# A recurrent layer followed by a mixture of experts: the first expert is settled in iteration 2, its weights are loaded in iterations 3 to 10, and units 4 and 5 are turned by TensorE

## The chip, the core and the metric

The kernel runs on one core of one Trainium2 chip. The metric is the device time of one execution in microseconds (us), here the median of three runs.

## What is computed

A linear recurrence with decay runs over 4 sequences of 768 tokens with 8 heads of 48 values, and its output (3072 tokens of 384 values) goes through a mixture of 8 experts, one expert for each token:

```python
for t in range(S):                      # recurrence: B 4, H 8, S 768, D 48
    cur = einsum('bhd,bhe->bhde', u * k[t], v[t])
    y[t] = einsum('bhd,bhde->bhe', r[t], state + cur)
    state = w * state + einsum('bhd,bhe->bhde', k[t], v[t])
logits = x @ w_gate + modality_bias[modality_id]   # x: y as 3072 x 384
e_idx = argmax(logits); gate_w = softmax(logits)[e_idx]
out[mask_e] = gate_w * (relu(x[mask_e] @ w1[e]) @ w2[e])   # e of 8, F 1024
```

## The kernel before

The tokens are cut into 24 **units** of 128 (chunk c of sequence b). The loop `for i in range(NU - 1)` in `run` is a software pipeline written out by hand: each engine executes its instructions in the order in which this loop issues them, and there is no scheduler behind it. In iteration i TensorE turns keys of unit i+2 (`keys_turned`, tile pkT), computes the scores of unit i+1 (`scores`, psc), then the output and the state of unit i (`values`, py and pst). VectorE masks scores (`causal`, at), adds the parts of the output of unit i-1 (`token`, py) and makes keys with decay (`keys`, kc). ScalarE copies states (st), scales values (`own`, dv) and makes the sum of squares of `token` (row). GpSimd makes rc, rk and kt. pst has one buffer, so `values` of unit i waits until ScalarE has taken the state of unit i-1 out of it. The psc, pkT and pxT tiles share four buffers.

SyncE (SP) issues the loads: per iteration `turned` (ud, of unit i+5) and `lines` (kv, of unit i+4). All go through one queue, in order, and an entry that waits holds up those behind it. `pace` makes SP wait for a value that VectorE has written.

Each finished unit is turned so that features lie on partitions, for the gate. `flip` does it by a DMA transpose (xT from row). For units in `RAISED`, `raised` does it on TensorE instead, with six 128x128 transposes into pxT two iterations later, and `flipped` copies pxT to xT on ScalarE. `logits` of the first group (units 0 to 3) stands at the end of iteration 5.

The experts' weights are of float32. They come into `raw` in halves of 256 KB (`half`, twelve for the first expert) and need six sums of squares (`norm` q, ScalarE into junk), two scale factors (`scales`, a matmul, a reduction wtotw and three small VectorE operations) and six `split`s: `wide` on ScalarE makes whi, `fine` on VectorE makes wlo. The first expert is chosen before the tokens are counted, by a poll (`first_order`): from the modality of the tokens and the bias it estimates which expert gets most tokens, and writes the order of the experts to `ctl`. SP reads the first of them from there before the first half is loaded.

Small work is threaded between the large by `fill()`: a list of generators of which each call runs one step. There are nine such calls in an iteration. `plan(i, f)` puts f at the end of iteration i, `begin[i]` and `mid[i]` put it inside. O is 8. From iteration 13 on the first expert's products (`s_up`, tile phs; `s_down`, pos) run between the units.

Of the kernel before, what the change touches and what calls it, by code (L numbers as in the profile page):

```python
# [9 lines left out]
F32 = mybir.dt.float32  # L10
# [8 lines left out]
P = 128  # L19
# [3 lines left out]
NT = B * S  # L23
# [25 lines left out]
RAISED = range(6, 12)  # L49
# [16 lines left out]
class _Kernel:  # L66
# [134 lines left out]
    def setup2(self):  # L201
# [10 lines left out]
        pt = self.ps_r.tile([P, 512], F32, tag="r", name="pswg")  # L212
# [19 lines left out]
        mf, mp = pt[:, 64 : 64 + NTT], c.tile([P, 1], F32, name="modp")  # L232
        self.polled = pt, mp, bias
        nc.scalar.activation(mf, mod.rearrange("p (t w) -> p t w", w=2)[:, :, 0], AF.Copy, accum_out=mp)
        yield
# [474 lines left out]

    def first_order(self):

        c, v = self.c, self.nc.vector
        pt, mp, bias = self.polled
        one = slice(0, 1)
        new = lambda name, shape: c.tile(shape, F32, name=name)
        b2 = bias.rearrange("p (m e) -> p m e", m=2)
        n1, rev, best1, perm = new("n1", [P, 1]), new("rev16", [P, E]), new("best1", [P, E]), new("perm0", [P, E, E])
        self.perm0 = perm
        square = lambda ap: ap.rearrange("p (a b) -> p a b", b=E)  # L720
        top, gr = pt[:, 384:386], square(pt[:, 128 : 128 + E * E])
        best0, by, rank, t = (pt[:, o : o + E] for o in range(400, 400 + 4 * E, E))
        self.nc.tensor.matmul(pt[:, 1:2], self.ones, mp, start=True, stop=True)
        v.reduce_max(top, b2, axis=AX.X)
        yield
        self.nc.scalar.activation(rev, self.rev, AF.Copy, scale=1 / 16)
        self.nc.scalar.activation(rev, self.rev, AF.Copy, scale=1 / 16)
        v.tensor_tensor(best0, b2[:, 0], top[:, :1].to_broadcast([P, E]), ALU.is_equal)
        yield
        self.nc.scalar.copy(n1, pt[:, 1:2])  # L730
        v.tensor_tensor(best1, b2[:, 1], top[:, 1:].to_broadcast([P, E]), ALU.is_equal)
        yield
        v.tensor_sub(by, best1, best0)
        yield
        v.scalar_tensor_tensor(best1, best0, float(NT), rev, ALU.mult, ALU.add)
        yield
        v.scalar_tensor_tensor(rev, by, n1, best1, ALU.mult, ALU.add)
        yield
        v.scalar_tensor_tensor(best0, by, n1, best1, ALU.mult, ALU.add)
        yield  # L740
        v.tensor_tensor(gr, rev.unsqueeze(1).to_broadcast([P, E, E]), best0.unsqueeze(2).to_broadcast([P, E, E]), ALU.is_gt)
# [12 lines left out]
        self.nc.scalar.copy(self.ctl[:, :E], eid)  # L754
# [394 lines left out]
    def run(self):  # L1149
# [34 lines left out]
        def half(q):  # L1184
            if q == 0:
                self.eid = nc.sync.value_load(self.ctl[:, :1], min_val=0, max_val=E - 1)
            if 0 <= q < 2 * NQ:
                self.load(self.eid, 2 * NQ, q)
# [12 lines left out]
        plan(1, lambda: fills.append(routing))  # L1201
        plan(3, lambda: fill(99))
        plan(3, lambda: fills.append(self.first_order()))
# [45 lines left out]
        for i in range(NU - 1):  # L1249
# [16 lines left out]
            if i == O + 5:  # L1266
                self.settled_state(i - 1)
# [7 lines left out]
            if i != O + 5:  # L1275
                each(i - 1, self.settled_state)
# [52 lines left out]
            if i != O + 5:  # L1329
                self.values(i)  # L1330
# [229 lines left out]
```

## Time and profile before

| what | value |
|---|---|
| median of three runs | 344.19 us (343.73 to 344.73) |
| the profiled execution | 343.19 us |
| its span, first to last instruction | 341.3 us |
| TensorE matmul busy | 322.7 us, 95% of the span |
| VectorE, ScalarE, GpSimd busy | 213.3, 180.1, 160.5 us |
| granted TensorE clock over the span | 0.997 |

The share of an engine is an average over stages. Busy time of TensorE counts matmuls whose ends are modelled, so that short waits between them hide in it. An iteration is told here from the first scores matmul of one unit to that of the next; iteration 2 begins at 19.52 us, iteration 14 ends at 100.18.

### The profile page before, as it was taken

The numbers are of one execution on the slowest core, as the hardware profiler recorded it, in microseconds if no ns is written. First come the engines' busy times: TensorE is split into PE (matmuls) and PEld (weight loads), VectorE is DVE, ScalarE is ACT, GpSimd is POOL, SyncE is SP. The second block draws the span as 40 slices with busy tenths as digits, with TensorE's granted clock in tenths as the row PEclk, the third lists the DMA queues.
The fourth block names the chain that finished last, engine by engine and source line by source line (L and its number), as shares of the span: only waits on it lengthen the run. The fifth ranks groups of instructions, "written<-read, shape, count | busy, mean of one in ns | idle before, by whom it ended". The sixth has DMA issues, their size and how long they took to land. (4 is left out here: it accounts for less than half of the span.)

```text
span 341.3 us, 15249 instructions
## 1 busy us (share of the span) xinstructions
PE 322.7 (95%) x5459; PEld 262.8 (77%) x5459; DVE 213.3 (63%) x745; ACT 180.1 (53%) x482; POOL 160.5 (47%) x237
## 2 busy tenths in 40 slices
PE   7999998889899999899999999999999999999992
PEld 3788897778778888687887778886888887777771
DVE  7868987489997997587758732268322332334950
ACT  7787788578766568367532222265222224553820
POOL 8978779688739786526268411112122111211211
PEclk9999999999999999999999999999999999999998
DMA  6766999667659999995345632217611121112110
GB/s 187 237 165 161 169 250 301 181 224 169 182 139 234 195 281 285 235 131 147 71 130 175 190 96 65 47 46 249 195 46 46 47 69 23 46 52 64 37 46 5
DMA packets 58013, 47.93 MB, mean 140 GB/s; under 512 B 42344, under 2 KB 50807, under 8 KB 57712
## 3 DMA queue, kind: packets, MB, share of 16 engines
q1 hardware_dynamic: 54768, 37.85, 46.9%
q0 software_dynamic: 3200, 9.47, 7.7%
q8 instruction: 30, 0.49, 0.6%
q14 instruction: 15, 0.12, 0.1%
HBM read 27.21 MB, written 11.83 MB: 114 GB/s over the span
## 5 line engine op out<-in xcount | busy, mean ns | idle before, releaser
L1051 PEld LDWEIGHTS <-whi 128*128 128x128 f16 x1248 | 72.4, 98 | 3.8 <-issue 0.9
L1060 DVE SCALAR_TENSOR_TENSOR hl<-phb,hh 128x256 f16<-128x256 f32 (+1 forms) x48 | 24.4, 508 | 68.3 <-ACTq L1491 68.3
L1114 PEld LDWEIGHTS <-hh 128*128 128x128 f16 x416 | 39.1, 98 | 27.6 <-issue 2.2
L1051 PE MATMUL phb<-mxT,whi 128*128 128x128 f16 x768 | 50.8, 219 | 0.0
L431 ACT ACTIVATE dv<-kv,d 128x48 f32<-128x48 f32 x172 | 43.1, 325 | 0.4 <-DVE d L419 0.2
L1055 ACT ACTIVATE hh<-phb 128x256 f16<-128x256 f32 (+1 forms) x48 | 21.5, 455 | 32.6 <-PE phb L1051 21.9
L1051 PEld LDWEIGHTS <-wlo 128*128 128x128 f16 x624 | 37.7, 98 | 0.0
L1020 POOL TENSOR_TENSOR seenb<-otb,putb 128x1 int32<-128x1 int32 x16 | 4.4, 275 | 64.0 <-ACTq L1491 51.9
L451 DVE TENSOR_TENSOR at<-psc,mask 128x512 f32<-128x512 f32 x48 | 31.9, 682 | 1.9 <-PE psc L445 1.8
L364 POOL TENSOR_TENSOR rc<-ud,powr 112x512 f32<-112x512 f32 (+1 forms) x25 | 31.0, 1243 | 0.7 <-DMA ud<-in_pd 0.5
L1114 PEld LDWEIGHTS <-hl 128*128 128x128 f16 x208 | 19.4, 98 | 15.3 <-issue 2.5
L1011 ACT ACTIVATE otb<-po,fac 128x384 f32<-128x384 f32 x16 | 9.3, 580 | 39.5 <-PE phb L1051 36.1
L688 POOL DMA_INDIRECT rows<-row,posi x24 | 25.0, 1042 | 10.8 <-DVE base L664 3.1
L445 PE MATMUL psc<-rc,kc 64*64 64x128 f32 (+1 forms) x768 | 27.1, 276 | 2.3 <-issue 1.5
L1051 PE MATMUL phb<-mxT,wlo 128*128 128x128 f16 x384 | 29.3, 219 | 0.0
L1114 PE MATMUL po<-whi,hl 128*128 128x384 f16 x136 | 28.0, 326 | 1.2 <-PEq L1556 0.7
L1114 PE MATMUL po<-whi,hh 128*128 128x384 f16 x136 | 27.7, 326 | 0.5 <-ACT hh L1055 0.4
L1114 PE MATMUL po<-wlo,hh 128*128 128x384 f16 x136 | 27.6, 326 | 0.0
L1051 PE MATMUL phs<-mxT,whi 128*128 128x128 f16 x432 | 27.2, 219 | 0.0
L445 PEld LDWEIGHTS psc<-rc,kc 64*64 64x64 f32 (+1 forms) x768 | 20.9, 132 | 7.9 <-issue 4.2
L482 PE MATMUL py<-kv,at 128*64 128x48 f32 x768 | 26.5, 221 | 0.0
L997 DVE SCALAR_TENSOR_TENSOR wlo<-raw,ws,whi 128x1024 f16<-128x1024 f32 (+1 forms) x20 | 25.0, 1277 | 1.4 <-issue 0.6
(287 smaller groups left out, 636.0 us busy)
## 6 DMA issues: line engine op xcount, KB each, us to landing
kv<-in_pt SPq DMA_DIRECT2D x21, 384.0 KB
ud<-in_pd SPq DMA_DIRECT2D x10, 384.0 KB
raw<-in_w SPq DMA_DIRECT2D x12, 256.0 KB
raw<-in_w SPq DMA_DIRECT2D x6, 512.0 KB
raw<-in_w SPq DMA_DIRECT2D x2, 1536.0 KB, 6.3
ud<-in_pd SPq DMA_DIRECT2D x14, 192.0 KB
rows<-pad SPq DMA_DIRECT2D x10, 193.0 KB
rt<-in_pt SPq DMA_DIRECT2D x7, 192.0 KB
```

What stands on the lines that cost most here:

```text
L364: nc.gpsimd.tensor_mul(u["rc"][:TOP, s], u["rT"][:TOP, s], self.powr[:TOP, s])
L431: nc.scalar.activation(u["dv"][:, sl], u["v"][:, sl], AF.Copy, scale=u["d"][:, h : h + 1])
L445: nc.tensor.matmul(u["ps"][j][s, pr * P : (pr + 1) * P], u["kc"][r, pr, s], u["rc"][r, pr, :], start=True, stop=True)
L451: nc.vector.tensor_mul(u["at"][:, j * NPR : (j + 1) * NPR, :], u["ps"][j].rearrange("p (q t) -> p q t", q=NPR), self.mask.unsqueeze(1).to_ ...
L482: nc.tensor.matmul(py[t, sl], u["at"][:, j * NPR + pr, t], u["v"][:, sl], start=c == h == 0, stop=h == H - 1, skip_group_check=True)
L688: i = nc.gpsimd.indirect_dma_start(out=self.rows, out_offset=bass.IndirectOffsetOnAxis(ap=u["posi"][:, b : b + 1], axis=0), in_=u["row"][: ...
L997: self.nc.vector.scalar_tensor_tensor(self.wlo[:, sl], self.raw[:, sl], sc, self.whi[:, sl], ALU.mult, ALU.subtract)
L1011: self.nc.scalar.activation(ot, po[:, :DM], AF.Copy, scale=gf[:, t : t + 1])
L1051: self.nc.tensor.matmul(ph[:, q * P : (q + 1) * P], w[:, c0 : c0 + P], self.xT[:, xq, t * P : (t + 1) * P], start=i == q == 0, stop=i == l ...
L1055: self.nc.scalar.activation(self.hh[:, f0 : f0 + fb, t * P : (t + 1) * P], p3, AF.Relu)
L1060: self.nc.vector.scalar_tensor_tensor(self.hl[:, f0 : f0 + fb, r], p3, 0.0, self.hh[:, f0 : f0 + fb, r], ALU.max, ALU.subtract)
L1114: self.nc.tensor.matmul(po[:, :DM], h[:, f, t * P : (t + 1) * P], w[:, c0 : c0 + DM], start=first, stop=last)
```

## The change

- `RAISED` begins at 4 and not at 6: units 4 and 5 are turned by TensorE in iterations 6 and 7, and their two DMA transposes, in iterations 5 and 6 on SP, go.
- The poll is taken apart. `first()` settles the first expert alone, writes `ctl[0]`, and runs at the head of the chain of small work, from iteration 2 on. The rest of `setup2` follows it, and then the rest of the order. Before, `setup2` came first and the poll began in iteration 4.
- The twelve halves are issued by a table, in iterations 3 to 10 (2, 1, 2, 1, 1, 2, 2, 1); before, two in each of iterations 6 to 11.
- The norms stand in iterations 5, 7, 8, 9, 10 and 11; before in 7 to 12. The splits stand in 9, 10, 11, 12 and two in 13; before in 10, 11, 12 and three in 13.
- `scales` of w1 stands in iteration 9 and not in 10; that of w2 in 12 and not inside `values` of iteration 13. The special order of iteration 13 goes with it.

```diff
-RAISED = range(6, 12)
+RAISED = range(4, 12)
...
-        self.polled = pt, mp, bias
-        nc.scalar.activation(mf, mod.rearrange("p (t w) -> p t w", w=2)[:, :, 0], AF.Copy, accum_out=mp)
-        yield
...
+    def first(self):
+        nc, c, v = self.nc, self.c, self.nc.vector
+        _, bias, mod = self.raw_in
+        pt = self.polled
+        new = lambda name, shape, dt=F32: c.tile(shape, dt, name=name)
+        top, n, part, ck, best, e0 = new("btop", [P, 2]), new("npoll", [P, 2]), new("ckpart", [P, E]), new("ck0", [P, E]), new("ckbest", [1, 1]), new("eid00", [1, 1])
+        self.ck0, mp, one = ck, new("modp", [P, 1]), slice(0, 1)
+        nc.scalar.activation(pt[:, 64 : 64 + NT // P], mod.rearrange("p (t w) -> p t w", w=2)[:, :, 0], AF.Copy, accum_out=mp)
+        nc.tensor.matmul(pt[:, 1:2], self.ones, mp, start=True, stop=True)
+        v.reduce_max(top, bias.rearrange("p (m e) -> p m e", m=2), axis=AX.X)
+        yield
+        nc.scalar.copy(n[:, 1:2], pt[:, 1:2])
+        nc.scalar.activation(n[:, 0:1], pt[:, 1:2], AF.Copy, scale=-1.0, bias=float(NT))
+        yield
+        two = [pt[:, 400 + E * m : 400 + E * m + E] for m in range(2)]
+        for m in range(2):
+            v.tensor_scalar(two[m], bias[:, m * E : (m + 1) * E], top[:, m : m + 1], n[:, m : m + 1], ALU.is_equal, ALU.mult)
+            yield
+        v.scalar_tensor_tensor(part, two[0], 16.0, self.rev, ALU.mult, ALU.add)
+        yield
+        v.scalar_tensor_tensor(ck, two[1], 16.0, part, ALU.mult, ALU.add)
+        yield
+        v.reduce_max(best, ck[one], axis=AX.X)
+        yield
+        v.scalar_tensor_tensor(two[0][one], ck[one], best, self.idx[one], ALU.is_equal, ALU.mult)
+        yield
+        v.reduce_sum(e0, two[0][one], axis=AX.X)
+        yield
+        v.tensor_copy(self.ctl[:, :1], e0)
+        v.scalar_tensor_tensor(two[0], two[1], 16.0, part, ALU.mult, ALU.add)
+        yield
...
-        def half(q):
-            if q == 0:
-                self.eid = nc.sync.value_load(self.ctl[:, :1], min_val=0, max_val=E - 1)
-            if 0 <= q < 2 * NQ:
+        halves = {3: (0, 1), 4: (2,), 5: (3, 4), 6: (5,), 7: (6,), 8: (7, 8), 9: (9, 10), 10: (11,)}
+
+        def half(i, at):
+            for q in halves.get(i, ())[at : at + 1]:
+                if q == 0:
+                    self.eid = nc.sync.value_load(self.ctl[:, :1], min_val=0, max_val=E - 1)
                 self.load(self.eid, 2 * NQ, q)
...
-        plan(1, lambda: fills.append(routing))
-        plan(3, lambda: fill(99))
-        plan(3, lambda: fills.append(self.first_order()))
+        plan(1, lambda: fills.append(chain(self.first(), routing, self.first_order())))
...
-        for q in range(3):
-            plan(O - 1 + q, norm(q))
-        begin[O + 2] = lambda: scales("w1", 0, O + 2)
-        for q in range(3):
-            plan(O + 2 + q, split(q))
-            plan(O + 2 + q, norm(3 + q))
-            plan(O + 5, split(3 + q))
-        mid[O + 5] = lambda: self.values(O + 5, lambda: (scales("w2", 1, O + 6), self.undo()))
+        norms = {}
+        for i, q in ((5, 0), (7, 1), (8, 2), (9, 3), (10, 4), (11, 5)):
+            norms.setdefault(i, []).append(q)
+        begin[9] = lambda: scales("w1", 0, 9)
+        begin[12] = lambda: (scales("w2", 1, 12), self.undo())
+        for i, qs in ((9, (0,)), (10, (1,)), (11, (2,)), (12, (3,)), (13, (4, 5))):
+            for q in qs:
+                plan(i, split(q))
+        for i, qs in norms.items():
+            for q in qs:
+                plan(i, norm(q))
```

What stands in `first_order` behind the poll is unchanged but for its first lines, which now use ck0 of `first`.

SP, iteration 3, before: ud and kv are the loads of `turned` and `lines`, ut a table.

```order
L333 DMA ud_85<-in_pd 96x512
L343 DMA kv_91<-in_pt 128x2x384
L572 DMA_TRANSPOSE xT_403<-row_402 128x6x128
L1205 DMA ut<-in_u 128x384
L333 DMA ud_86<-in_pd 96x512
```

And now:

```order
L330 DMA ud_85<-in_pd 96x512
L1197 TENSOR_LOAD ctl
L1197 ISA x2
L966 ISA
L966 DMA raw<-in_w 128x512
L340 DMA kv_91<-in_pt 128x2x384
L966 ISA
L966 DMA raw<-in_w 128x512
L569 DMA_TRANSPOSE xT_403<-row_402 128x6x128
L1213 DMA ut<-in_u 128x384
L330 DMA ud_86<-in_pd 96x512
```

The read of `ctl` and the first two halves now stand among the loads of iteration 3, ahead of a kv load and a transpose.

ScalarE, iteration 2, before: wd and tri are tables of `setup2`, st the state of unit 1.

```order
L519 ACTIVATE row_402,ssq_404<-py_444 128x384
L217 ACTIVATE wd<-id_150,w_186 112x112
L534 COPY st_99<-pst_461 64x4x48
L217 ACTIVATE wd<-id_150,w_186 112x112
L534 COPY st_99<-pst_461 48x4x48
L217 ACTIVATE wd<-id_150,w_186 112x112 x2
L220 CAST tri<-mask 128x128
L431 ACTIVATE dv_535<-kv_91,d_510 128x48 x4
```

And now:

```order
L516 ACTIVATE row_402,ssq_404<-py_444 128x384
L716 ACTIVATE pswg,modp<-mod 128x24
L531 COPY st_99<-pst_461 64x4x48
L720 COPY npoll<-pswg 128x1
L721 ACTIVATE npoll<-pswg 128x1
L531 COPY st_99<-pst_461 48x4x48
L428 ACTIVATE dv_543<-kv_91,d_518 128x48 x4
```

The two npoll copies read a matmul of TensorE on modp; wd and tri move behind them, to iteration 3.

ScalarE, end of iteration 12 to end of 13, before: whi is `wide`, junk is `norm`.

```order
L992 ACTIVATE whi<-raw,ws 128x1024
L961 ACTIVATE junk,wssq<-raw 128x1024
L542 COPY st_98<-pst_1960 64x4x48
L542 COPY st_98<-pst_1960 48x4x48
L519 ACTIVATE row_2055,ssq_2057<-py_1935 128x384
L580 COPY xT_1421<-pxT_1988 128x768
L431 ACTIVATE dv_2088<-kv_92,d_2061 128x48 x4
L552 ACTIVATE row_2055<-py_1935,sx_2058 128x384
L1055 ACTIVATE hh<-phs_0_2015 128x4x128
L463 ACTIVATE st_98<-st_99,w_186 112x2x96 x2
L992 ACTIVATE whi<-raw,ws 128x1024 x3
```

And now:

```order
L1000 ACTIVATE whi<-raw,ws 128x1024
L516 ACTIVATE row_2082,ssq_2084<-py_1965 128x384
L539 COPY st_98<-pst_1990 64x4x48
L539 COPY st_98<-pst_1990 48x4x48
L577 COPY xT_1444<-pxT_2017 128x768
L428 ACTIVATE dv_2117<-kv_92,d_2088 128x48 x4
L549 ACTIVATE row_2082<-py_1965,sx_2085 128x384
L1063 ACTIVATE hh<-phs_0_2044 128x4x128
L460 ACTIVATE st_98<-st_99,w_186 112x2x96 x2
L1000 ACTIVATE whi<-raw,ws 128x1024 x2
```

No norm is left in iteration 12, and two splits are left at the end of 13.

## Rows read from the trace of the kernel before

In the windows view a row gives the stretch, its length, then busy time and records (x) of PE, PEld, DVE, ACT and POOL, the granted clock share, the DMA share and GB/s.

**Rows 1.** Page, queues by kind: packets, MB, share of 16 engines.

```profile
q8 instruction: 30, 0.49, 0.6%
```

**Rows 2.** Busy by window; windows are iterations 2, 3, 6, 8 to 14.

```profile
19.52:23.74 4.22, 4.22 (x104) 3.48 (x104) 2.63 (x10) 4.16 (x16) 3.48 (x3) 1.00 0.73 187
23.74:27.31 3.57, 3.57 (x101) 3.21 (x100) 2.85 (x11) 3.07 (x13) 2.22 (x2) 1.00 0.46 112
...
39.06:44.37 5.31, 4.91 (x133) 4.42 (x133) 4.86 (x18) 3.90 (x14) 4.36 (x7) 1.00 1.04 184
...
49.65:54.64 4.99, 4.99 (x139) 4.63 (x138) 4.22 (x14) 3.91 (x15) 3.72 (x3) 1.00 1.05 343
54.64:62.09 7.45, 5.76 (x163) 5.29 (x162) 4.62 (x21) 6.72 (x19) 6.96 (x7) 1.00 0.86 270
62.09:69.75 7.66, 5.71 (x141) 4.92 (x140) 4.38 (x18) 4.04 (x9) 4.63 (x6) 1.00 0.65 182
69.75:75.97 6.22, 5.58 (x151) 4.97 (x150) 5.29 (x18) 5.09 (x13) 5.52 (x6) 1.00 0.64 193
75.97:81.44 5.47, 4.80 (x136) 4.27 (x135) 4.84 (x18) 4.59 (x14) 3.35 (x4) 1.00 0.90 195
81.44:90.62 9.18, 9.18 (x227) 8.80 (x226) 8.72 (x28) 8.14 (x19) 8.63 (x8) 1.00 0.53 179
90.62:100.18 9.56, 8.14 (x139) 5.63 (x136) 9.53 (x21) 4.02 (x14) 3.45 (x4) 1.00 0.49 122
```

**Rows 3.** Busy by window, between three idle places of PE.

```profile
42.41:58.16 15.75, 14.06 (x383) 12.86 (x383) 13.05 (x45) 13.42 (x46) 12.97 (x14) 1.00 0.99 280
58.16:64.28 6.12, 4.59 (x129) 4.15 (x129) 1.92 (x9) 4.62 (x14) 5.12 (x6) 1.00 0.81 239
```

**Rows 4.** Timeline of PE, iterations 9 and 10: start, length, work, idle before.

```profile
58.16 0.30 PE L475 MATMUL py<-st,rc 112*64 112x96 f32 x2 [1.69 <-issue]
...
64.28 0.88 PE L445 MATMUL psc<-rc,kc 48*64 48x128 f32 x21 [1.53 <-issue]
```

**Rows 5.** Timeline of DVE, iterations 9 to 14.

```profile
53.55 0.57 DVE L504 TENSOR_TENSOR py<-py,dv 128x384 f32<-128x384 f32 x1
...
65.30 0.16 DVE L979 TENSOR_REDUCE wtotw<-py 128x1 f32<-128x3 f32 x1 [4.16 <-PE py L976]
...
70.26 0.55 DVE L504 TENSOR_TENSOR py<-py,dv 128x384 f32<-128x384 f32 x1
...
83.19 0.56 DVE L504 TENSOR_TENSOR py<-py,dv 128x384 f32<-128x384 f32 x1
...
90.32 5.21 DVE L997 SCALAR_TENSOR_TENSOR wlo<-raw,ws,whi 128x1024 f16<-128x1024 f32 x3
```

**Rows 6.** Timeline of PE, iteration 14.

```profile
93.19 0.48 PE L1114 MATMUL pos<-wlo,hh 128*128 128x384 f16 x2 [0.71 <-DVE wlo L997]
```

**Rows 7.** Timeline of ACT, iterations 2 and 3.

```profile
18.94 0.19 ACT L519 ACTIVATION_READ_ACCUMULATOR row<-py 128x1 f32 x1
...
25.19 0.32 ACT L534 COPY st<-pst 48x192 f32<-48x192 f32 x1
```

**Rows 8.** Timeline of PE, iterations 2 and 3.

```profile
19.52 1.10 PE L445 MATMUL psc<-rc,kc 64*64 64x128 f32 x32
...
25.74 0.57 PE L496 MATMUL pst<-kv,kt 128*64 128x48 f32 x15
```

**Rows 9.** Timeline of DVE, iteration 4.

```profile
30.65 0.16 DVE L731 TENSOR_TENSOR best<-bias,pswg 128x8 f32<-128x8 f32 x1 [1.43 <-ACT n L730]
```

**Rows 10.** Timeline of PE, iteration 7 into 8.

```profile
48.78 0.49 PE L565 MATMUL pxT<-id,row 128*128 128x128 f16 x6
49.12 0.60 PE L352 MATMUL pkT<-id,kv 128*112 128x128 f32 x4
```

**Rows 11.** Timeline of ACT, iteration 11.

```profile
71.97 0.80 ACT L580 COPY xT<-pxT 128x768 f16<-128x768 f16 x1
...
75.16 1.06 ACT L961 ACTIVATE junk<-raw 128x1024 f16<-128x1024 f32 x1
```

More of the change, by code (lines that the diff above doesn't have):

```diff
@@ L211, in setup2 @@
         yield
-        pt = self.ps_r.tile([P, 512], F32, tag="r", name="pswg")
+        pt = self.polled = self.ps_r.tile([P, 512], F32, tag="r", name="pswg")
         nc.tensor.matmul(pt[:, :1], self.ones, ssq, start=True, stop=True)
@@ L231, in setup2 @@
         NTT = NT // P
-        mf, mp = pt[:, 64 : 64 + NTT], c.tile([P, 1], F32, name="modp")
-        self.polled = pt, mp, bias
-        nc.scalar.activation(mf, mod.rearrange("p (t w) -> p t w", w=2)[:, :, 0], AF.Copy, accum_out=mp)
-        yield
+        mf = pt[:, 64 : 64 + NTT]
         mg = pt[:, 96 : 96 + NTT]
@@ L711, in first_order @@
     def first_order(self):
-        c, v = self.c, self.nc.vector
-        pt, mp, bias = self.polled
+        c, v, pt = self.c, self.nc.vector, self.polled
         one = slice(0, 1)
         new = lambda name, shape: c.tile(shape, F32, name=name)
[L717 to L741, printed above, removed]
+        perm = self.perm0 = new("perm0", [P, E, E])
@@ L742, in first_order @@
+        gr = pt[:, 128 : 128 + E * E].rearrange("p (a b) -> p a b", b=E)
+        ck, rank, t = (pt[:, o : o + E] for o in (400, 408, 416))
+        v.tensor_tensor(gr, self.ck0.unsqueeze(1).to_broadcast([P, E, E]), ck.unsqueeze(2).to_broadcast([P, E, E]), ALU.is_gt)
         yield
@@ L753, in first_order @@
         yield
-        self.nc.scalar.copy(self.ctl[:, :E], eid)
+        self.nc.scalar.copy(self.ctl[:, 1:E], eid[:, 1:])
         self.settled = new("settled", [P, E])
@@ L1274, in run @@
             each(i, self.taken) if i else None
-            if i != O + 5:
-                each(i - 1, self.settled_state)
+            each(i - 1, self.settled_state)
             if i - 2 in RAISED:
@@ L1281, in run @@
                 each(i + 5, self.turned)
-            half(2 * (i - O) + 4)
+            half(i, 0)
             for j in range(2):
@@ L1309, in run @@
                     each(i + 4, self.lines)
-                half(2 * (i - O) + 5)
+                half(i, 1)
                 each(i + 3, self.own_lines)
@@ L1328, in run @@
             fill()
-            if i != O + 5:
-                self.values(i)
+            self.values(i)
             if up is not None:
```

2 lines of the change are left out of this document (removed).

## The prediction

> **What bounds the kernel now.** I read the page first, then a table of busy time by iteration, and then the timelines of the iterations that stand out. TensorE runs in program order through everything, so the question in each stage is what its next matmul waits for. Iteration 8 shows how good it gets: 4.99 us, with TensorE busy throughout [rows 2]. Iterations 9 to 12 do the same work per unit, with logits in one and small work between, and last 7.45, 7.66, 6.22 and 5.47, 26.80 together, while TensorE is busy for 5.76 + 5.71 + 5.58 + 4.80 = 21.85 [rows 2]. Iteration 14 lasts 9.56 with 8.14 busy [rows 2]. These are the places where the change can win.
>
> Three causes are to be seen there. First, TensorE stands still for 1.69 and 1.53 us, and the profile names no releaser, only "issue" [rows 4]. Between an earlier, shorter such place at 42.41 and the first of these lie 383 + 383 = 766 matmuls and weight loads, and to the next 129 + 129 = 258 [rows 3]: three times some 255, and once. The page has an instruction queue that moved 0.49 MB in 30 packets, 16.3 KB each [rows 1]. I read it, as an inference, as code that is fetched block by block and comes late. Until then the DMA engines had been at a share of 0.99 [rows 3]. Second, VectorE waits 4.16 us for the matmul of `scales` in iteration 10 [rows 5], which stands behind the second of these stalls. Third, the weights' splits: a fine split must end before the next `token`, and the tokens of iterations 11 and 13 are 83.19 - 70.26 = 12.93 apart, 6.47 an iteration [rows 5], against 4.99 in iteration 8. Three fine splits in a row take 5.21 us [rows 5], and TensorE waits 0.71 for one [rows 6], and as long again once more in the same iteration.
>
> **The change part by part**, against the profiled execution's 343.19 us.
>
> *A, the poll in iteration 2.* Its VectorE operations are small. Its price is the wait: the two npoll copies on ScalarE need a matmul that stands behind the scores of iteration 2. ScalarE is done with its sum of squares at 18.94 + 0.19 = 19.13 [rows 7], then come two short operations, to about 19.6. The scores end at 19.52 + 1.10 = 20.62 [rows 8], and the poll's matmul follows, so that ScalarE is idle until about 20.9: 1.3 us. VectorE's next keys, masks and token queue behind the same value, and by my count of what stands between, token 2 comes about 1.1 us late, and ScalarE is idle a second time, by 0.9. In iterations 2 and 3 ScalarE is busy for 4.16 + 3.07 = 7.23 of 7.79 us [rows 2], so it has 0.56 to spare. 1.3 + 0.9 - 0.56 is 1.6 us of lag. It reaches TensorE through pst: ScalarE's last copy of the old state ends at 25.19 + 0.32 = 25.51 [rows 7], and the matmuls that overwrite it start at 25.74 [rows 8], 0.2 later. From below: the old poll goes, where VectorE waited 1.43 us in iteration 4 [rows 9]; if that cost TensorE 1.0 and the new one nothing, the part gains 1.0. From above: both idle times in full and some of the work that moves into iteration 3, 2.6. I take **+1.6**, since ScalarE's row of iteration 2 shows it nearly full.
>
> *B, five halves in iterations 3 to 5.* A half is 256 KB; at the 343 GB/s of iteration 8 [rows 2] it takes 0.76 us, so the five take 3.8 us. In iteration 3 the DMA share is 0.46 of 3.57 us [rows 2], so its two halves, 1.5 us, nearly fit. Iteration 6 shows the other end: share 1.04 at only 184 GB/s [rows 2], with a DMA transpose in it. Of the units' transposes, that of unit 3 still comes in iteration 4, and the logits of iteration 5 wait for it. The kv and ud loads behind the halves on SP have an iteration of lead or more, and the read of `ctl` costs no wait of its own, since `pace` waits for a later VectorE operation next to it. Lower end 0; upper end two late code blocks like those of rows 4, 3.2. I take **+0.7**, nearer to the row of iteration 3.
>
> *C, units 4 and 5 on TensorE.* Six transposes take 0.34 us until the next matmul starts (48.78 to 49.12) [rows 10], on TensorE's path: 0.68 for two units. ScalarE gets two copies of 0.80 [rows 11] in iterations 6 and 7, and a norm of 1.06 [rows 11] moves ahead into iteration 5. In iteration 6 it is busy 3.90 of 5.31 [rows 2], which hides one copy; where a norm stands too, in 7, I count 0.3. Against it stand the two DMA transposes, and iteration 6's idle 5.31 - 4.91 = 0.40 on TensorE [rows 2], which I count as won. **+0.6**, between 0 and +1.5.
>
> *D, iterations 9 to 12.* The load in iterations 6 to 8 falls from six halves to four, and both transposes there go, so that the stalls of rows 4 should go or shrink; `scales` no longer stands behind one. What remains is a loop of ScalarE and VectorE: token, squares, state copies, dv, high, wide split, fine split, next token, which takes 6.47 us as measured above. There are now four such iterations instead of three. VectorE's span from token to token over iterations 9 to 12 was 83.19 - 53.55 = 29.64 [rows 5]; four loops of 6.47 are 25.9, so the part wins 29.64 - 25.9 = 3.7, **-3.8** with the small gain that no norm is left in iteration 12. The most would be TensorE's idle time, 26.80 - 21.85 = 4.95; the least, with both stalls back, 3.8 - 3.2 = 0.6. The second `scales` now costs VectorE some 0.5 us in iteration 12; I let it lie beside TensorE's work.
>
> *E, iteration 14.* Two fine splits instead of three stand ahead of `s_down`. TensorE's idle 9.56 - 8.14 = 1.42 [rows 2] goes: **-1.4**. At least one of the two waits goes, 0.7; at most a whole fine split, 5.21 / 3 = 1.74.
>
> The moved SP entries, the rest of `setup2` behind the poll and the special order of iteration 13 I cost at nothing: wghl, lb and perm0 are wanted from iteration 5 on, a whole iteration after they are made, and iteration 13 has TensorE busy for 9.18 of 9.18 us [rows 2]. If that cover were gone, the small work would cost VectorE some tenths in iteration 4. Everything behind iteration 14 is issued in the program's order, so a shift there should be carried to the end.
>
> Sum: 1.6 + 0.7 + 0.6 - 3.8 - 1.4 = -2.3, so 340.9 for the profiled execution. It lies 1.00 below the median of 344.19; against that median the forecast is **341.9**.
>
> **Rivals.** *R1, the stalls move forward (slower).* Late code blocks come back in iterations 3 to 5. With 201 matmuls and weight loads in iteration 3 and 325 in iteration 9 [rows 2] TensorE crosses some three blocks there. If each costs 1.69 [rows 4], B is 5.1 instead of 0.7: 341.9 + 4.4 = 346.3. For it: five halves and the transposes meet there. Against it: DMA shares of 0.73 and 0.46 in iterations 2 and 3 [rows 2]. It decides above 1.3 us a block: 3 x 1.3 = 3.9 = 0.7 + 2.3 + about 1.
>
> *R2, the stalls stay (about no change).* If the idle places of rows 4 do not come from the DMA load, or if two halves in iterations 8 and 9 with the indirect writes are enough to make them, D loses 3.2: 341.9 + 3.2 = 345.1. Against it speak the spacing by 255 and the full DMA engines before them; for it, that iteration 8 itself, share 1.05 [rows 2], has no such stall. [...]
>
> *R3, the poll is free (faster).* If TensorE is far enough ahead in iterations 2 to 5, A is -1.0 instead of +1.6: 341.9 - 2.6 = 339.3. For it: TensorE loses time in iteration 5 already now. Against it: ScalarE's full row in iteration 2.
>
> **How the numbers follow.** Forecast 0.49, R1 0.12, R2 0.17, R3 0.22. A measurement of this kernel can tell about 0.3% from no change, 1.03 us: faster is below 343.2, slower above 345.2. Of the forecast's 0.49 I count 0.42 as faster and 0.07 as same, of R2 0.11 as same and 0.06 as slower. Faster: 0.42 + 0.22 = 0.64; same 0.18; slower 0.12 + 0.06 = 0.18. The range takes in R3 with half a microsecond below it and R2 with half above: 338.8 to 345.6; the half of R1 beyond it and the ends of D are left out.
>
> **What would show it.** A: in iteration 2 ScalarE idle before npoll by over 1 us, and iteration 6 starting 1 to 2 us after 39.06. B: no idle "issue" place over 0.5 us on TensorE before 40 us. C: pxT rows in iterations 6 and 7 with 0.34 us each. D: no "issue" idle over 1 us in iterations 9 to 12, VectorE's wait for `scales` under 2 us, tokens 6.3 to 6.6 apart. E: iteration 14 near 8.1 us. The forecast is wrong if iteration 6 starts 4 us late, or if 9 to 12 still last over 25.5 us.

## The result and the profile after

The changed kernel is slower, by half a per cent: 345.39 us in the median of 20 runs, against 344.01 for 20 runs of the kernel before beside them. The ratio is 1.0052 (95% interval 1.0029 to 1.0076). The forecast was 341.9, faster, with a range of 338.8 to 345.6. The profiled execution of the changed kernel took 344.49 us, its span is 342.8.

Busy time of the changed kernel in six stages: iterations 2 to 4, 5 to 8, 9 to 12, 13 and 14, 15 to 21, the rest; and a stretch of its own (columns as in [rows 2]):

```profile
19.41:34.42 15.01, 13.27 (x338) 11.49 (x337) 10.38 (x37) 11.32 (x45) 9.89 (x9) 1.00 0.72 174
34.42:56.85 22.43, 21.67 (x589) 19.65 (x588) 19.32 (x66) 19.82 (x67) 17.17 (x19) 1.00 0.81 239
56.85:82.61 25.76, 22.92 (x587) 20.76 (x587) 22.89 (x78) 20.35 (x51) 20.43 (x20) 0.93 0.64 174
82.61:99.31 16.70, 16.70 (x363) 14.27 (x361) 16.52 (x44) 10.38 (x29) 14.01 (x12) 1.00 0.73 172
99.31:152.84 53.53, 53.53 (x1082) 45.53 (x1081) 43.35 (x147) 35.08 (x112) 34.65 (x43) 1.00 1.02 233
152.84:342.70 189.86, 179.66 (x2243) 141.61 (x2241) 87.27 (x337) 68.95 (x139) 48.36 (x104) 0.99 0.31 83
70.79:74.21 3.42, 3.42 (x62) 3.09 (x56) 2.50 (x12) 2.69 (x10) 3.11 (x5) 0.50 0.40 119
```

The same stages of the trace on which the prediction rests, the third and the last:

```profile
54.65:81.44 26.79, 21.85 (x586) 19.44 (x585) 19.12 (x73) 20.43 (x53) 20.45 (x21) 1.00 0.76 211
...
154.78:341.30 186.52, 179.19 (x2243) 141.65 (x2241) 86.72 (x338) 69.02 (x140) 48.57 (x104) 1.00 0.31 85
```

At the start of the last stage the changed kernel is 154.78 - 152.84 = 1.94 us ahead, nearly the 2.3 that the forecast had. Behind it, where the change touches nothing, it loses 189.86 - 186.52 = 3.34. The jobs show how. ScalarE's hh in one job of that first trace, and then in the changed kernel (start, length, work, idle time before):

```profile
223.36 0.60 ACT L1055 ACTIVATE hh<-phb 128x512 f16<-128x512 f32 x1 [1.42 <-PE phb L1051]
224.52 0.38 ACT L1055 ACTIVATE hh<-phb 128x256 f16<-128x256 f32 x1 [0.56 <-PE phb L1051]
```

```profile
222.87 0.60 ACT L1063 ACTIVATE hh<-phb 128x512 f16<-128x512 f32 x1 [1.42 <-PE phb L1059]
224.74 0.38 ACT L1063 ACTIVATE hh<-phb 128x256 f16<-128x256 f32 x1 [1.27 <-PE L1122]
```

A job is one pass of the loop behind the last unit, which takes tokens of one expert through its two products; hh is what lies between these. The second hh comes 1.87 us behind the first and not 1.16, although TensorE's matmuls for it are equally far along: they end 0.74 us behind the first hh in that trace and 0.73 here. In a job that changes the expert this reaches TensorE: the first hh of the next job came 9.29 us behind this one in that trace (232.65) and comes 9.93 behind it here (232.80). Jobs without a change of expert follow each other at 7.95 in both.

### The profile page after: what moved, and what is told of

Read it like the earlier page. It is cut to its first block, busy times and chain, and to the rows that moved or that the text cites. A ratio compares the mean times of both kernels' runs of the same rounds, so it can differ in the third digit from the quotient of the medians.

```text
span 342.8 us, 15268 instructions
## 1 busy us (share of the span) xinstructions
PE 325.1 (95%) x5471; PEld 264.7 (77%) x5471; DVE 216.1 (63%) x748; ACT 180.6 (53%) x483; POOL 161.8 (47%) x237
## 5 line engine op out<-in xcount | busy, mean ns | idle before, releaser
L1028 POOL TENSOR_TENSOR seenb<-otb,putb 128x1 int32<-128x1 int32 x16 | 4.4, 273 | 66.7 <-ACTq L1498 53.2
L685 POOL DMA_INDIRECT rows<-row,posi x24 | 26.5, 1105 | 11.0 <-DVE base L661 3.1
L442 PE MATMUL psc<-rc,kc 48*64 48x128 f32 (+1 forms) x768 | 27.8, 280 | 0.2
L1005 DVE SCALAR_TENSOR_TENSOR wlo<-raw,ws,whi 128x1024 f16<-128x1024 f32 (+1 forms) x20 | 25.9, 1313 | 1.3 <-issue 0.6
L442 PEld LDWEIGHTS psc<-rc,kc 48*64 48x64 f32 (+1 forms) x768 | 21.3, 134 | 6.2 <-issue 2.8
```

Of the source, the lines that this page charges most:

```text
L442: nc.tensor.matmul(u["ps"][j][s, pr * P : (pr + 1) * P], u["kc"][r, pr, s], u["rc"][r, pr, :], start=True, stop=True)
L685: i = nc.gpsimd.indirect_dma_start(out=self.rows, out_offset=bass.IndirectOffsetOnAxis(ap=u["posi"][:, b : b + 1], axis=0), in_=u["row"][: ...
L1005: self.nc.vector.scalar_tensor_tensor(self.wlo[:, sl], self.raw[:, sl], sc, self.whi[:, sl], ALU.mult, ALU.subtract)
```

## First question: does the late hh belong to the change?

*x1_after_again* is the changed kernel unchanged, *x2_before_again* and *z4_before_third* are the kernel before unchanged.

> The changed kernel, unchanged, a second time. In its first trace the whole forecast gain was there at the end of the unit loop (first scores of unit 23 at 153.34 us against 155.28) and 3.4 us were lost behind it: ScalarE's second hh in each job came 1.88 us behind the first instead of 1.16, and one hh at 185.01 us 1.8 us after its products were done. While GpSimd worked at an indirect write, the trace has 5.5 semaphore updates per us in the jobs, against 31 before. Theory K: this belongs to the program (where its code or its buffers lie); then the second trace shows 1.88 again and the ratio to the kernel before is 1.005. Theory L: it belongs to one loading of a program, whatever it is; then the second trace can show 1.16, and the ratio comes near 0.995 where it does. Rival C: code blocks of ScalarE come late there; then 1.88 again, but with no change in the semaphore updates.

> The kernel before, unchanged, with a trace of its own. Theory K: second hh 1.16 us behind the first in every job without a change of expert, semaphore updates during indirect writes as dense as in its first trace (31 per us), ratio 1.000. Theory L: the trace can show 1.88 us and few updates, and then a time up to 3 us above 343.2.

> The kernel before, a third trace. If its first trace was the odd one: second hh in the jobs 1.8 to 1.9 us behind the first as in the second trace, few semaphore updates in GpSimd's indirect writes, and TensorE's two idle places of iterations 9 and 10 again of other lengths (1.69 and 1.53 in the first trace, under 0.7 in the second). If both ways are common: 1.16 again.

Ratios to the kernel before, run beside it each time: x1 1.004 (1.0009 to 1.0071), x2 1.0011 (0.9978 to 1.0044); z4, one execution, 344.42 us. The expectations measure stages from other marks than this text does, so that their lengths differ from those below by some tenths. The second trace of the kernel before, the same six stages:

```profile
19.34:32.36 13.02, 13.01 (x339) 11.40 (x338) 9.29 (x34) 11.35 (x46) 9.24 (x8) 1.00 0.65 156
32.36:54.03 21.67, 21.00 (x576) 19.12 (x576) 19.12 (x66) 17.30 (x61) 17.58 (x19) 1.00 0.88 230
54.03:78.15 24.12, 21.76 (x585) 19.36 (x584) 19.95 (x74) 20.01 (x53) 20.41 (x21) 1.00 0.86 241
78.15:96.90 18.75, 17.61 (x363) 14.46 (x361) 18.26 (x49) 12.16 (x32) 12.09 (x11) 1.00 0.57 147
96.90:151.31 54.41, 53.72 (x1081) 45.64 (x1080) 44.12 (x149) 35.41 (x114) 35.20 (x43) 1.00 1.05 228
151.31:341.00 189.69, 179.69 (x2243) 141.58 (x2241) 89.02 (x337) 68.94 (x139) 48.27 (x104) 1.00 0.31 84
```

The first trace was an odd one. The kernel before has the late hh too, and a last stage of 189.69 us; so have all 18 traces taken after the first, of whatever kernel (189.7 to 190.2). Counted in the trace's list of semaphore updates, GpSimd's indirect writes in the jobs have some 30 updates per us beside them in the first trace and 5 to 7 in all the others. Part of this is missing records: the same program has 511 updates by VectorE, and the list has 511 in the first trace and 473 in x2's. That some updates come late is seen in the hh: 1.14 us behind the end of its matmuls in the changed kernel, 0.42 in the first trace. Theory L comes nearest, with the odd way seen once only; K falls, since x2 and z4 are the very program of the first trace. C gets no support, because the updates are few wherever the hh is late. Why one execution was spared is open.

The second odd thing is the two idle places of [rows 4]. The second trace of the kernel before has none over 0.4 in iterations 9 and 10; the third (TensorE's timeline):

```profile
57.41 0.30 PE L475 MATMUL py<-st,rc 112*64 112x96 f32 x2 [1.13 <-issue]
...
62.98 0.88 PE L445 MATMUL psc<-rc,kc 48*64 48x128 f32 x21 [0.58 <-issue]
```

So 1.69 and 1.53 us are one draw of something that varies from execution to execution. Its place does not vary. Counted in TensorE's recorded matmuls and weight loads from the start of the program, all 27 "issue" places of over 0.35 us in iterations 5 to 12, in 15 of the 19 traces, stand at 1713, 1971, 2225, 2477 to 2481, 2733 to 2735 or 2987 to 2989: some 255 apart, whatever the edit, and at most of these counts a trace has no such place. This bears out the prediction's reading of blocks of code, as far as places go; what sets the length is open. The spared tail (3.2 us) and the long idle places offset each other: the span was 341.3, and 341.0 in x2. Lengths of the stages in us:

| stage | before, three traces | changed, two traces |
|---|---|---|
| iterations 2 to 4 | 13.04, 13.02, 13.03 | 15.01, 15.02 |
| 5 to 8 | 22.09, 21.67, 21.93 | 22.43, 23.30 |
| 9 to 12 | 26.79, 24.12, 25.67 | 25.76, 25.67 |
| 13 and 14 | 18.75, 18.75, 18.75 | 16.70, 16.70 |
| 15 to 21 | 54.59, 54.41, 53.61 | 53.53, 53.66 |
| the rest | 186.5, 189.7, 190.0 | 189.9, 189.7 |

With the second and third trace of before, the means differ by +1.99, +1.07, +0.82, -2.05, -0.42 and about 0: +1.4 us. The measured ratios make it 1.8 (the 20 executions) and 1.4 (x1). The experiments take these apart.

## The poll (part A)

*y2* is the kernel before with `first()`, the chain and nothing else. *y1* is the changed kernel with the poll's sum moved up:

```diff
         nc.scalar.activation(wq, wg, AF.Square, accum_out=ssq)
-        yield
         pt = self.polled = self.ps_r.tile([P, 512], F32, tag="r", name="pswg")
+        mp = c.tile([P, 1], F32, name="modp")
+        nc.scalar.activation(pt[:, 64 : 64 + NT // P], mod.rearrange("p (t w) -> p t w", w=2)[:, :, 0], AF.Copy, accum_out=mp)
+        yield
         nc.tensor.matmul(pt[:, :1], self.ones, ssq, start=True, stop=True)
+        nc.tensor.matmul(pt[:, 1:2], self.ones, mp, start=True, stop=True)
         yield
...
-        self.ck0, mp, one = ck, new("modp", [P, 1]), slice(0, 1)
-        nc.scalar.activation(pt[:, 64 : 64 + NT // P], mod.rearrange("p (t w) -> p t w", w=2)[:, :, 0], AF.Copy, accum_out=mp)
-        nc.tensor.matmul(pt[:, 1:2], self.ones, mp, start=True, stop=True)
+        self.ck0, one = ck, slice(0, 1)
```

> The kernel before with the early poll alone (part A): loads, norms, splits and transposes where they were. Theory A: iteration 6 starts 1.5 to 2.0 us later than in the second trace of before (38.55 by the same marks), and as nothing is won for it, the time is 345.2 to 345.6. Rival (the early halves cost it): iteration 6 within 0.4 us, time 343.6 to 344.

> The changed kernel, with the poll's sum made at the end of iteration 0 (ScalarE) and its matmul at the end of iteration 1, so that the two npoll copies of iteration 2 find it done. Theory A (the new poll costs what ScalarE waits for this matmul): in the second trace of the kernel before, iteration 6 starts 2.5 to 2.9 us earlier than in the two traces of the changed kernel; of that some 1.5 us come back here, and the time falls from 345.1 to about 343.6. Rival: the lag comes from the early halves' transfers or from the work that moved into iteration 3, and no more than 0.3 us come back.

y2: ratio 1.007 (1.0045 to 1.0094), 2.4 us for the poll alone; iterations 2 to 4 last 15.02 (window):

```profile
19.60:34.62 15.02, 13.24 (x338) 11.47 (x337) 10.38 (x37) 11.33 (x45) 9.88 (x9) 1.00 0.57 141
```

y1: 13.05, the whole lag gone, yet the ratio is 1.0011 (0.998 to 1.0042; median 345.41 beside 344.26). ScalarE in iteration 2 of the changed kernel, then of y1:

```profile
20.86 0.16 ACT L720 COPY npoll<-pswg 128x1 f32<-128x1 f32 x1 [1.43 <-PE pswg L717]
```

```profile
19.29 0.15 ACT L721 COPY npoll<-pswg 128x1 f32<-128x1 f32 x1
```

A is what the prediction said, a wait for a matmul behind the scores, and y2 shows it in the time. What y1 does not give back is, in its trace, a wait that the lag had covered. TensorE's timeline in y1, and a window behind that wait:

```profile
40.59 0.31 PE L590 MATMUL pr<-wghl,xT 128*128 128x16 f16 x6 [2.50 <-DMA xT<-row]
```

```profile
32.85:58.80 25.95, 23.11 (x589) 20.98 (x588) 20.35 (x66) 20.78 (x69) 17.20 (x19) 0.93 0.71 210
40.74:44.15 3.41, 3.41 (x48) 2.84 (x45) 1.57 (x7) 2.57 (x7) 0.86 (x1) 0.50 0.78 245
```

The logits of iteration 5 wait for unit 3's DMA transpose. The wait is 2.50 us, and behind it the granted clock is 0.50 for 3.41 us; iterations 5 to 8 last 25.95. Not every execution seems to have it: of y1's twelve, eight had a mean clock of 0.982 to 0.987, as the traced one, and took 344.5 to 347.7 us; the other four had 0.990 to 0.995 and took 342.6 to 343.9. *z1* puts the halves later, `halves = {i: (2 * (i - 5), 2 * (i - 5) + 1) for i in range(5, 11)}`, with norms in 6 to 11 and y1's poll.

> The changed kernel with the poll's sum early (as in y1_poll_sum_earlier) and the twelve halves two by two in iterations 5 to 10, one iteration earlier than in the kernel before; norms in 6 to 11, splits as changed. There a 2.5 us wait of TensorE for the DMA transpose of unit 3 (logits, iteration 5) had eaten what the early poll's sum gave back. Theory B (the halves of iterations 3 and 4 stand ahead of that transpose): the wait goes or falls under 0.5 us, no clock fall behind it, and the ratio falls from 1.001 to 0.995 to 0.998. Rival (any early half delays it, or the transposes are late of themselves): the wait stays above 1 us and the ratio stays at 1.001 or above.

The wait is gone, and the ratio is 0.9993 (0.9967 to 1.0019). Iterations 5 to 8 and 9 to 12 of z1:

```profile
32.97:55.49 22.52, 21.71 (x588) 19.75 (x588) 19.28 (x66) 19.62 (x66) 16.96 (x18) 1.00 0.90 243
55.49:82.35 26.86, 24.10 (x586) 21.65 (x585) 23.41 (x78) 20.68 (x53) 20.69 (x20) 0.87 0.70 185
```

So the halves of iterations 3 and 4 did hold up the transpose in y1's trace, by 2.5 us, where A no longer made TensorE late (z1 also moves the other halves and one norm); with the lag the same wait is 0 to 0.94 us (changed, x1, x3, y3). Over all executions the two ratios do not tell z1 from y1. A wait of 0.2 to 0.6 us for this transpose stands in the traces of w2, z3 and w4 (below) too, whose halves come later, so early halves are not its only cause.

## Units 4 and 5 (part C)

*x3* and *x4* change only `RAISED`, in the changed kernel back to `range(6, 12)`, in the kernel before to `range(4, 12)`.

> The changed kernel with units 4 and 5 turned by DMA as before (part C undone). By the forecast's own terms TensorE gets 0.68 us back (2 x 0.34) and two DMA transposes come back in iterations 5 and 6, among five early halves: iteration 8 starts within 0.6 us of the changed kernel's, earlier if TensorE's share was the price, later if the transposes hold up loads. Theory K: the program differs by 12 transposes, so that the slow hh may go (1.16) and the time fall to 342; theory L: no relation to the edit.

> The kernel before with part C alone: units 4 and 5 turned by TensorE. If the two idle places of 1.69 and 1.53 us in iterations 9 and 10 came from the DMA load of iterations 6 to 8, one transpose less in iteration 6 should shorten the first; if from the spacing of code by some 255 instructions alone, both move 24 instructions earlier with their lengths kept. Time: 0.6 us slower by the forecast's term C, 0.9 faster if one of the two idle places halves.

x3: 1.0052 (1.002 to 1.0083); x4: 0.9991 (0.9963 to 1.0018). x3 cannot be told from the changed kernel, nor x4 from the kernel before. In x4's trace iterations 5 to 8 last 22.49, 0.6 above the mean of before, and 9 to 12 last 23.87, with one idle place of 1.09 us. The forecast's +0.6 for the transposes is found in that stage, but not in the time. Iteration 8 of x3 starts 32.44 us behind iteration 2, between the two traces of the changed kernel (32.07 and 32.91). The idle place of 1.09 us in x4 is at 2987 of the count above: it stays with the count and not with a place in the program, and the one at 2479 is not there at all.

## Norms and splits (parts D and E)

*y3* puts them back where they were in the otherwise changed kernel, with the scales at the starts of iterations 10 and 13.

```diff
-        for i, q in ((5, 0), (7, 1), (8, 2), (9, 3), (10, 4), (11, 5)):
+        for i, q in ((7, 0), (8, 1), (9, 2), (10, 3), (11, 4), (12, 5)):
...
-        for i, qs in ((9, (0,)), (10, (1,)), (11, (2,)), (12, (3,)), (13, (4, 5))):
+        for i, qs in ((10, (0,)), (11, (1,)), (12, (2,)), (13, (3, 4, 5))):
```

> The changed kernel with norms in 7 to 12, splits in 10, 11, 12 and three in 13, scales in 10 and 13, as before (parts D and E undone); poll, halves and units 4 and 5 as changed. Theory: the new places of norms and splits win about 1.8 us in iteration 14 and lose about 1.7 in iterations 10 and 11, where TensorE waits 0.64 and 1.01 us in a row and its granted clock then falls to 0.5 for 3.4 us; so here the clock stays at 1.00 up to 339 us, iterations 9 to 12 get 1 to 1.7 us shorter, iteration 14 is 9.4 again, and the time is within 0.5 us of 345.1. Rival (the lag at the start sets all): iterations 9 to 12 keep their length, and the time is 1.8 us longer, 347.

Ratio 0.9999 (0.9968 to 1.003): by the ratios 1.4 to 1.8 us faster than the changed kernel, which neither the theory (no change) nor the rival (slower) had; the theory is nearer. Its iterations 9 to 12, then 13 and 14:

```profile
58.04:82.48 24.44, 22.67 (x586) 20.59 (x585) 20.16 (x71) 18.82 (x49) 20.23 (x21) 0.93 0.71 187
82.48:100.07 17.59, 16.95 (x364) 14.31 (x362) 16.85 (x49) 12.27 (x32) 12.61 (x11) 1.00 0.54 153
```

Iterations 9 to 12 are 1.3 us shorter, as the theory had it. Two parts of it failed: the clock fell here too, behind an "issue" place of 1.44 us, and iteration 14 lasts 8.65 and not 9.4, since y3 keeps the plain order of iteration 13 (below).

Why do four iterations with a split last 25.6 to 25.8 in all five traces with the new places and the changed halves? VectorE's tokens (L501) and fine splits of iterations 9 to 12 in the changed kernel, and GpSimd beside the first and the last split:

```profile
55.79 0.57 DVE L501 TENSOR_TENSOR py<-py,dv 128x384 f32<-128x384 f32 x1
...
62.07 2.40 DVE L1005 SCALAR_TENSOR_TENSOR wlo<-raw,ws,whi 128x1024 f16<-128x1024 f32 x1
64.39 0.55 DVE L501 TENSOR_TENSOR py<-py,dv 128x384 f32<-128x384 f32 x1
...
69.71 1.26 DVE L1005 SCALAR_TENSOR_TENSOR wlo<-raw,ws,whi 128x1024 f16<-128x1024 f32 x1
70.90 0.55 DVE L501 TENSOR_TENSOR py<-py,dv 128x384 f32<-128x384 f32 x1
...
75.94 1.35 DVE L1005 SCALAR_TENSOR_TENSOR wlo<-raw,ws,whi 128x1024 f16<-128x1024 f32 x1
77.22 0.55 DVE L501 TENSOR_TENSOR py<-py,dv 128x384 f32<-128x384 f32 x1
...
82.56 2.55 DVE L1005 SCALAR_TENSOR_TENSOR wlo<-raw,ws,whi 128x1024 f16<-128x1024 f32 x1
85.03 0.55 DVE L501 TENSOR_TENSOR py<-py,dv 128x384 f32<-128x384 f32 x1
```

```profile
62.09 1.28 POOL L361 TENSOR_TENSOR rc<-ud,powr 112x512 f32<-112x512 f32 x1
...
82.73 1.28 POOL L361 TENSOR_TENSOR rc<-ud,powr 112x512 f32<-112x512 f32 x1
```

The splits of 9 and 12 take 1.1 to 1.3 us longer, about as long as GpSimd's rc, which begins beside them. In x2 a split and kt meet the other way round: the split takes 1.26, and GpSimd's kt, which mostly takes 1.00, takes 2.08:

```profile
65.80 1.26 DVE L997 SCALAR_TENSOR_TENSOR wlo<-raw,ws,whi 128x1024 f16<-128x1024 f32 x1
```

```profile
65.85 2.08 POOL L371 TENSOR_TENSOR kt<-kv,wtok 128x384 f32<-128x384 f32 x1
```

All 19 traces show the same: each of the 21 fine splits of over 2.3 us before 100 us has a whole rc or kt within it, and in 17 traces a kt that begins within 0.1 us behind a split takes 2.06 to 2.12. The recorded starts do not tell which of the two takes longer: the split at 82.56 begins 0.17 us ahead of rc and takes 2.55, beside an rc of 1.28; the one at 65.80 begins 0.05 ahead of kt, and there the kt takes longer. No run took GpSimd's work away from there, so that GpSimd's work is the cause is read from rows and not shown by an edit. With the waits for the scales (1.62 us in iteration 9) added, VectorE's tokens stand 8.60, 6.51, 6.32 and 7.81 us apart over these four iterations.

*z2* is z1 without a split in iteration 9: `((10, (0,)), (11, (1,)), (12, (2, 3)), (13, (4, 5)))`.

> As z1_halves_5_to_10, and no split in iteration 9: splits in 10, 11, two in 12, two in 13. Theory D (four iterations with a wide and a fine split last 4 x 6.47 = 25.9 us where three last 24.2): iterations 9 to 12 fall from 25.8 to about 24.5 us and iteration 14 keeps 7.6; ratio 0.003 below that of z1. Rival (the two splits in iteration 12 cost there what is saved in 9): 25.5 and the same ratio.

Ratio 1.0006 (0.9983 to 1.003), iterations 9 to 12 last 25.58, and 13 and 14 last 17.64: the rival, by the ratio and by the length that it named. z1's own trace had 26.86 and not the 25.8 expected, with a granted clock of 0.50 for 6.83 us in iterations 10 and 11. The split of iteration 10 in z2 takes 3.17 us and the first of iteration 12 takes 2.55.

*y4* fills two waits of TensorE in the changed kernel. They belong to the transposes of unit 9, which `run` issues in iteration 11, and by the marks of this text stand at the end of iteration 10:

```profile
68.33 0.34 PE L562 MATMUL pxT<-id,row 128*128 128x128 f16 x3 [0.64 <-ACT row L549]
69.68 0.34 PE L562 MATMUL pxT<-id,row 128*128 128x128 f16 x3 [1.01 <-DVE row L553]
```

Behind them its clock was 0.50 for 3.42 us (last row of the first fence).

```diff
         for q in range(2 * DC):
+            for _ in range({0: 11, DC: 18}.get(q, 0) if i == 9 else 0):
+                self.nc.tensor.transpose(u["pt"][:, q, :], self.id16, self.id16)
```

> The changed kernel with 11 and 18 transposes of the identity ahead of the two groups of transposes of unit 9 (iteration 11), where TensorE waits 0.64 and 1.01 us: at 0.056 us each they fill these waits. If the waits make the clock fall, the 3.4 us at 0.5 that follow (70.8 to 74.2 us in one trace, 71.4 to 74.8 in the other) go, and up to 1.7 us of TensorE's time come back: 343.4 to 345. Rival (the clock falls for something else, or ScalarE and VectorE are the bound there anyway): no change or up to 0.5 us slower.

Windows of y4, iterations 9 to 12 and the stretch in which the clock had fallen:

```profile
57.45:83.14 25.69, 23.00 (x615) 20.92 (x614) 22.86 (x78) 20.27 (x51) 20.37 (x20) 1.00 0.61 173
70.79:74.21 3.42, 3.42 (x102) 3.07 (x101) 2.50 (x10) 2.26 (x10) 3.12 (x4) 1.00 0.33 93
```

The clock stays at 1.00, and nothing is won: 25.69 again, ratio 1.0042 (1.0017 to 1.0067). The changed kernel has a third wait, 0.74 us at 66.13, which is absent in y4's trace without being filled; but the mean clock is 0.994 or more in 9 of y4's 12 executions and in 3 of the changed kernel's 32, which speaks for the filled waits. So these waits do make the clock fall, and the fall of 3.42 us costs nothing there, because VectorE sets the pace: its tokens stand 8.63, 6.52, 6.32 and 7.81 us apart in y4, as in the changed kernel. A longer fall is another matter: behind the 6.83 us of z1 the last two of these are 6.86 and 8.19. What the fall costs behind y1's wait, where TensorE was the bound, no run took apart.

## Which part pays

*z3* and *w2* are one kernel: y1's poll, units 4 and 5 by TensorE, halves, norms and splits as before, the scales of w2 at the start of iteration 13. *w3* is z3 with `RAISED = range(6, 12)`, *w4* is z1 with the splits as before. *v1* is the kernel before with the plain order of iteration 13 alone, *w1* is v1 with `RAISED = range(4, 12)`:

```diff
-        mid[O + 5] = lambda: self.values(O + 5, lambda: (scales("w2", 1, O + 6), self.undo()))
+        begin[O + 5] = lambda: (scales("w2", 1, O + 5), self.undo())
...
-            if i == O + 5:
-                self.settled_state(i - 1)
...
-            if i != O + 5:
-                each(i - 1, self.settled_state)
+            each(i - 1, self.settled_state)
...
-            if i != O + 5:
-                self.values(i)
+            self.values(i)
```

> The early poll with its sum early, units 4 and 5 turned by TensorE, and halves, norms and splits where the kernel before has them. Theory A: with the sum early the poll costs nothing; and parts A and C together are worth 0 to 0.5 us against the kernel before (343.3 to 343.8 beside 343.6), not 2.3 us slower as the early poll alone. Rival: moving the poll costs by what it pushes into iterations 3 and 4, 345 or more.

> z3_early_poll_rest_as_before unchanged, a second time. If its 0.9969 stands, 0.995 to 0.999 again, and a trace that reaches unit 23's scores near 152 us; if that was chance, 1.000.

> z3 with units 4 and 5 turned by DMA as before, so that the early free poll and the plain order of iteration 13 are all that differs from the kernel before. If part C is worth about nothing (0.9991 alone, and 0.0012 between x1 and x3), the ratio is within 0.002 of z3's.

> z1 with the splits where the kernel before has them (10, 11, 12, three in 13), norms still in 6 to 11. Theory: what the new splits win in iteration 14 (1.8 us) they lose in iterations 9 to 12 (four loops with a split and not three), so that this ratio is within 0.002 of z1's 0.9993, with iterations 9 to 12 some 1.5 us shorter and iteration 14 near 9. Rival: the split in iteration 9 costs more than it wins, and this one comes to z3's 0.997.

> The kernel before with units 4 and 5 turned by TensorE and w2's scales at the start of iteration 13 in place of the special order there; poll, halves, norms and splits as before. In the traces iterations 13 and 14 last 18.4 us together in the kernel before and 17.3 where the scales stand so (y3, z3). If that is z3's gain, the ratio is 0.996 to 0.998 here too. If the early free poll is, this one stays at 0.999 to 1.001, as before with units 4 and 5 alone (0.9991).

> The kernel before with w2's scales at the start of iteration 13 in place of the special order there, and nothing else. Iterations 13 and 14 last 17.2 to 17.3 us together in every trace with that order (y3, z3, w1, w2, w3) and 18.4 in every trace without it; if this is what pays, the ratio is 0.994 to 0.997, 1.1 to 1.8 us below before. Rival: units 4 and 5 pay in w1; then 0.998 to 1.000 here.

| kernel | median us | before beside it | ratio | interval |
|---|---|---|---|---|
| z3 | 343.02 | 343.97 | 0.9969 | 0.9942 to 0.9995 |
| w2, the same | 342.52 | 343.81 | 0.9964 | 0.9932 to 0.9996 |
| w3 | 343.01 | 343.81 | 0.9970 | 0.9944 to 0.9997 |
| w4 | 344.94 | 343.81 | 1.0015 | 0.9987 to 1.0043 |
| v1 | 342.69 | 343.41 | 0.9962 | 0.9929 to 0.9996 |
| w1 | 342.16 | 343.81 | 0.9949 | 0.9926 to 0.9972 |

The ratio is not the quotient of the two medians; for v1 that would be 0.9979.

Iterations 13 and 14 of v1, then of w1 (windows):

```profile
78.48:96.07 17.59, 16.95 (x364) 14.31 (x362) 16.84 (x49) 12.28 (x32) 12.62 (x11) 1.00 0.59 158
```

```profile
78.82:96.39 17.57, 16.93 (x364) 14.32 (x362) 16.82 (x49) 12.27 (x32) 12.59 (x11) 1.00 0.55 154
```

18.75 has become 17.6 by the plain order, 1.16 us; v1's ratio makes its gain 1.3 (0.1 to 2.4). v1's trace alone would not have shown it at the end: its span is 341.0, as x2's, with 54.96 us in iterations 15 to 21, the longest of all. It is the five series with that order and the old splits (z3, w2, w3, v1, w1), all of them below 1, that carry the reading. The changed kernel's 16.70 has another 0.9 from two splits instead of three. All that z3, w2 and w3 win is found in the plain order: their poll, once free, adds nothing that these intervals can tell. w1 is faster than both kernels, 1.7 us below before and more than its expectation had, with two of the change's edits. w4 missed its range by a little: without the new splits it is 0.0022 slower than z1, within the intervals. The stages came as its theory said, 25.19 in iterations 9 to 12 (z1 26.86) and 9.02 in iteration 14; its trace, the slowest of its twelve executions, has a fallen clock from 39.47 to 42.88 us, and iterations 5 to 8 last 25.08.

## Why the prediction was wrong

- *A, right in kind.* Forecast +1.6; +1.99 in the traces, 2.4 alone in y2. ScalarE waits 1.43 us for the poll's matmul where 1.3 was said. R3's free poll exists (z3, w2, w3), but nothing shows of the 1.0 us that R3 had it win.
- *B and C, about right in the stage, in part by luck.* Forecast +1.3 together; +1.07 in iterations 5 to 8. That B was small there was owed to A. The prediction's sign for B, no "issue" place over 0.5 us before 40 us, failed at 26.89 us with 0.76. That place belongs to A: y2 has it, without early halves, and y1 and z1 do not. R1's late blocks did not come.
- *D, the step that failed.* Forecast -3.8; -1.0 against the first trace, +0.8 against the mean of the two others. Three things went wrong in it. The gain was taken as 29.64 - 25.9, VectorE's span from token to token, although TensorE's own four iterations were 26.80 [rows 2]; that difference alone left 0.9. The four loops were sized at 6.47 from the two iterations that had no scales, and they measure 8.60, 6.51, 6.32 and 7.81, 29.24 together: right for the two in the middle, and 2.1 and 1.3 too short for those with scales and with rc beside the split. And 3.2 us of "issue" in [rows 4] were read as a steady cost that a lighter load would remove. In the first trace of the changed kernel they are gone, as forecast, with none over 0.2 us in iterations 9 to 12, and the stage still lasts 25.76. The 29.64 had these places in it: the same span of VectorE is 26.59 in x2 and 28.12 in z4, so that against those the four loops are longer and not shorter. Added up over iterations 9 and 10, such places of over 0.3 us come to 0.4 to 3.2 in nine traces with halves in 6 to 11 (mean 1.4; z3's trace, 3.7 us above its median, is left out), and to 0 to 1.4 in the nine with earlier halves (mean 0.5). So a lighter load does seem to shorten them, by some 0.9 and not by 3.2, and the first trace stood at the upper end. R2, about no change, was the nearest rival in its sum, not in its reason: the stalls did not stay in the first trace of the changed kernel. Of the 19 traces 12 have no such place of over 1 us in iterations 9 and 10, while the trace on which the prediction rests has two; the spread between executions of one kernel is what the prediction did not have.
- *E, two thirds of it, beside a term that was put at nothing.* Forecast -1.4 for the splits; the stage gave -2.05, of which 0.9 from the splits and 1.16 from the special order of iteration 13, which the prediction had costed at nothing since TensorE was busy for 9.18 of 9.18 us in iteration 13. Most of that 1.16 comes out in iteration 14, 8.65 in v1 against 9.56: the three fine splits take 4.67 us there in one go, against 5.22 in x2. The first of them takes 2.82 in every trace with the special order, where a kt of GpSimd runs within it, and 1.5 in v1. The edit costed at nothing was the one that paid.
- *"Everything behind iteration 14 is issued in the program's order, so a shift there should be carried to the end."* Against the first trace 3.3 us were lost behind the unit loop; against the other two all but 0.4 was carried, and iterations 15 to 21 alone vary by more than that (53.2 to 55.0 us over the traces). The sentence holds as far as these traces can tell, and the reference was at fault.
- With the measured stages in place of the terms the sum is the +1.4 above. The prediction's own test, "9 to 12 still last over 25.5 us", caught it: 25.76.

## What to carry to other kernels

Before a forecast of under one per cent is hung on a stall in one trace, look at a second trace of the same kernel: here two anomalies of 3 us each, in opposite directions, left a span that differed by 0.3 from the next trace's. Take a gain from the engine whose end is the metric, and size a loop from every iteration that it will contain, with what GpSimd does beside it. When a lag is taken away, ask which wait it was covering. Give an edit that seems covered a run of its own: v1, the cheapest of these, held most of what there was to win.

## What the runs showed of the hardware

- While GpSimd worked at an indirect write, recorded semaphore updates were few in 18 of 19 traces (5 to 7 per us in the jobs, some 30 in the other), and a reader of TensorE's semaphore went on 0.7 us late. How many of the updates came late and how many records are missing is not told apart. In the jobs the recorded updates of TensorE come every 30 ns at best, while it makes two (a matmul and its weight load) in 56 ns.
- Waits of 0.64 and 1.01 us close together were followed by 3.42 us at a granted clock of 0.50; with matmuls in these waits the clock stayed at 1.00.
- TensorE's idle "issue" places of over 0.35 us in iterations 5 to 12 (27 in 19 traces) stand at counts of matmuls and weight loads some 255 apart, the same in every kernel; their lengths run from nothing to 2.41 us.
- A fine split took 2.38 to 3.18 us where a whole rc or kt of GpSimd ran within it; where it took 1.26 us beside a kt, that kt took 2.06 to 2.12 us and not 1.00.
